# A spectral filter with a gated causal convolution: one convolution block in seven on GpSimd

## The chip, the cores and the metric

The kernel runs on one core of a Trainium2 chip. The metric is the device time of one execution in microseconds; the median of three runs of the kernel before is 308.13 us (307.31 to 309.5). One more execution was recorded by the hardware profiler: it took 308.17 us, and its trace spans 306.3 us from the first to the last instruction.

## What is computed

Eight batches of 3200 x 256 go through a filter in the frequency domain (along the 3200), and then through a gated unit with a causal convolution of five taps, one weight for each tap and channel.

```python
X = np.fft.rfft(x, axis=1)
Y = X * (filt_r + 1j * filt_i)[None, :, :]
y = np.fft.irfft(Y, n=3200, axis=1)
yp = np.concatenate([np.zeros((8, 4, 256)), y], axis=1)
gate_pre = sum(conv_w[k] * yp[:, k:k + 3200, :] for k in range(5))
gate = 1.0 / (1.0 + np.exp(-gate_pre))
out = (gate * (y @ w_val)) @ w_out
```

## The kernel before

The transform of length 3200 is cut into 100 x 32. For each batch the work goes through these stages, named as the tasks in the code are named:

- `lx`: eight loads of x (200 KB each as bf16), issued on GpSimd (line 202), into a pool of ten buffers.
- `s1` / `so`: eight first-stage products on TensorE (line 467), each into a two-bank PSUM area, and their evacuation to the tile `so` by ScalarE or VectorE (lines 458 and 460, the two arms of the helper `copy`).
- `t`: four 32x32 transposes on VectorE (line 486).
- `s2` / `xs` / `z` / `ia` / `ue`: in seven pieces, the second-stage product (line 496), its evacuation `xs`, the multiplication with the filter on VectorE (line 512, `z`, both inputs in SBUF), the first inverse product (line 527) and its evacuation to `u`. The seventh piece is half as wide.
- `wr` / `lv`: from batch 1 on, `u` goes to a scratch in DRAM and comes back in another order as `vt`, with DMAs issued on SyncE (lines 550, 560 and 561). Batch 0 has transposes on VectorE instead (line 568).
- `ib` / `ye`: eight second inverse products (line 578), evacuated by ScalarE to `yt` (line 587), which holds a batch of y, channels on partitions, bf16, with four columns of zeros ahead (`ha`, a memset on GpSimd, line 594).
- Then for each of seven blocks of up to 512 positions (the seventh has 128): `cv`, the convolution as 20 matmuls of 64x64 diagonal weights `dg_t` (line 609); `ga`, its sigmoid on ScalarE from PSUM to `gt` (line 619); `vl`, the value product (line 628); `gv`, gate times value on VectorE (line 643); `op`, the output product (line 651); `oe`, its evacuation to `o`; `st`, the store of 512 KB issued on SyncE (line 666), from a pool of five buffers.

A convolution block needs all eight `ye` of its batch. There are four PSUM areas of two banks for all products. GpSimd cannot hand anything over in PSUM, and in this kernel it only loads, writes constants and makes memsets.

The order on each engine is made when the program is built. `Plan` holds every task with an engine (or two that it may go to), a cost, a rank and what it depends on; `run` goes through an estimated time and gives each free engine the ready task of lowest rank. The rank of a task of batch b is `8 * b + LAG[stage] + STEP[stage] * n`, with `FIRST` added for batch 0; `STAY` and `LEAN` add to the rank where TensorE would change its mode or where VectorE would take a task that ScalarE could take as well. Each engine then runs its list strictly in that order. Instructions on different engines wait for each other through semaphores.

The first 44 us hold the tables that are computed on the chip, the filter's load and batch 0. Batches then overlap: while batch b is convolved, batch b+1 goes through its filter and batch b+2 through its first stage.

Of the kernel before, what the change touches and what calls it, by code (L numbers as in the profile page):

```python
# [20 lines left out]
NV = 4 * NS  # L21
TURN = (0,)

LAG = dict(lx=-36, s1=-112.5, so=-60, t=188, pd=-44.5, s2=33.5, xs=111.5, z=-11, ia=44.5,
           ue=37.5, k=-47, ib=73, ye=38.5, cv=84, ga=-76.5, vl=75, gv=-70.5, op=82, oe=29)
FIRST = dict(lx=-69, s1=32.5, so=44.5, t=56.5, pd=-52, s2=8, xs=4.5, z=-13, ia=-16.5, ue=49.5,
             k=-34, ib=-10.5, ye=10.5, cv=10.5, vl=-27.5, gv=3, op=99.5, oe=-45.5)
CONV = 1.0
STEP = dict(lx=0.25, s1=0.8, so=1.4, t=0.8, s2=1.25, xs=0.4, z=2.35, ue=0.5, k=1.35, ib=0.15,
            ye=1.8, cv=0.1, ga=2.1, vl=0, gv=0.4, op=0.2, oe=0.2)  # L30
STAY, LEAN = 17.5, 12
RC = 4
NCH = R // RC
UCH = [(m, min(2, NM - m)) for m in range(0, NM, 2)]
BLK = 512
NB = 7
MAGIC = 12582912.0
SEM = dict(PE=0.2, ACT=0.13, DVE=0.13, none=0.0)


class Plan:
# [9 lines left out]
    def add(self, name, engines, rank, deps, emit, take=(), give=(), land=0.0, mode=None,  # L51
            ps=0, free=()):
        self.tasks[name] = dict(engines=engines, rank=rank, deps=deps, emit=emit, take=take,
                                give=give, land=land, mode=mode, ps=ps, free=free, slots=[])

    def places(self, n):
        if n == 0:
# [7 lines left out]
    def run(self):  # L65
        left = dict(self.tasks)
        users, need = {}, {}
        for n, t in left.items():
            need[n] = len(t["deps"])
            for d in t["deps"]:  # L70
                users.setdefault(d, []).append(n)
        ready_at = {n: 0.0 for n in left}
        free = {}
        mode = turn = None
        gives = []
        ready = {n for n in left if need[n] == 0}
        order = []
        now = 0.0
        while left:
            gives.sort(key=lambda v: v[0])  # L80
            while gives and gives[0][0] <= now + 1e-9:
                for pool in gives.pop(0)[1]:
                    if isinstance(pool, int):
                        self.slots.append(pool)
                    else:
                        self.room[pool] += 1
            best = None
            for n in ready:
                t = left[n]
                if ready_at[n] > now + 1e-9:  # L90
                    continue
                if self.places(t["ps"]) is None or any(self.room[p] < 1 for p in t["take"]):
                    continue
                for e, cost in t["engines"].items():
                    if free.get(e, 0.0) <= now + 1e-9:
                        away = e == "PE" and t["mode"] != mode
                        other = e == "DVE" and len(t["engines"]) > 1
                        key = (t["rank"] + (self.stay if away else 0.0)
                               + (self.lean if other else 0.0), cost)
                        if e == "DQ":  # L100
                            key = (ready_at[n] + (1e4 if t["mode"] == turn else 0.0), 0.0)
# [36 lines left out]
        return order  # L138
# [3 lines left out]
def kernel(  # L142
# [37 lines left out]
    dg_t = cpool.tile([128, 2, K, 64], BF16, name="dg_t")  # L180
    wv_t = cpool.tile([128, 2, D], BF16, name="wv_t")
    wo_t = cpool.tile([128, 2, D], BF16, name="wo_t")

    dpool = ctx.enter_context(tc.tile_pool(name="scr", bufs=2, space=bass.MemoryType.DRAM))
    pp = ctx.enter_context(tc.tile_pool(name="ps", bufs=1, space=bass.MemoryType.PSUM))
    ps_all = pp.tile([128, 4, 1024], FP32, name="ps")
    NXT = 10
    xpool = ctx.enter_context(tc.tile_pool(name="xin", bufs=NXT))
    sopool = ctx.enter_context(tc.tile_pool(name="s1o", bufs=1))
    tpool = ctx.enter_context(tc.tile_pool(name="s2i", bufs=1))  # L190
# [81 lines left out]
    def load_w():  # L272
        for dh in range(2):
            for r in range(2):
                ch = 128 * dh + 64 * r
                nc.gpsimd.dma_start(
                    out=wv_t[:, dh, :].rearrange("p (r h j) -> p h r j", r=2, h=2)[:, r],
                    in_=moe_w_val[128 * dh:128 * dh + 128, 128 * r:128 * r + 128]
                    .rearrange("p (h j) -> p h j", h=2))
                nc.gpsimd.dma_start(out=wo_t[64 * dh:64 * dh + 64, r, :],  # L280
                                    in_=moe_w_out[ch:ch + 64, :])

    def sp_setup():
        cw = g["cw"] = g1.tile([128, 2, K], FP32, name="cw")
# [9 lines left out]
                                      in_=f_t[p:p + 32, w, :, m0:m1, :])  # L294

    def cf_dve():
        idx = g1.tile([128, 2, 2, 32], FP32, name="idx")
        V.scalar_tensor_tensor(idx[...], g["k1f"][...], g["pcol"][:, 0:1], g["phf"][...],
                               op0=ALU.mult, op1=ALU.add)
        ts(idx[...], idx[...], 0.01, ALU.mult)  # L300
# [301 lines left out]
    def conv(b, c):  # L602
# [9 lines left out]
                                 start=(k == 0), stop=(k == K - 1))  # L612
        st["cv", b, c] = ps

    def gate(b, c):
        ps = st.pop(("cv", b, c))
        g = gpool.tile([128, 2, BLK], BF16, name="gt")
        w = width(c)
        nc.scalar.activation(g[:, :, 0:w], two_banks(ps, w), AF.Sigmoid)  # L619
        st["G", b, c] = g  # L620

    def val(b, c):
# [3 lines left out]
        for eh in range(2):  # L626
            for dh in range(2):
                nc.tensor.matmul(ps[:, 512 * eh:512 * eh + w],  # L628
                                 lhsT=wv_t[:, dh, 128 * eh:128 * eh + 128],
                                 rhs=y[:, dh, H + BLK * c:H + BLK * c + w],  # L630
                                 start=(dh == 0), stop=(dh == 1))
        st["vl", b, c] = ps
# [13 lines left out]
    def outp(b, c):  # L646
        gv_ = st.pop(("GV", b, c))
        ps = psum()
        for a in range(width(c) // 128):
            for eh in range(2):  # L650
                nc.tensor.matmul(ps[:, D * a:D * a + D],  # L651
                                 lhsT=gv_[:, eh, 128 * a:128 * a + 128], rhs=wo_t[:, eh, :],
                                 start=(eh == 0), stop=(eh == 1))
        st["op", b, c] = ps

# [7 lines left out]
    def store(b, c):  # L663
# [4 lines left out]
            in_=o[:, 0:w // 128 * D])  # L668


    plan = Plan(dict(xt=NXT, so=1, t=1, xs=3, z=3, u=1, e=2, v=1, y=2, g=NGB, gv=NGB, o=NOB), 4,
                stay=STAY, lean=LEAN)
    add = plan.add

# [7 lines left out]
    for b in range(B):  # L682
# [65 lines left out]
        add(f"ha{b}", {"POOL": 0.2}, at("ib"), [f"ye{b},0"], lambda e, b=b: halo(b))  # L748
        for c in range(NB):
            f = width(c) / BLK  # L750
            add(f"cv{b},{c}", {"PE": 1.08 * f}, at("cv", c),
                [f"ye{b},{j}" for j in range(NCH)] + [f"ha{b}", "dg0", "dg1"],
                lambda e, b=b, c=c: conv(b, c), ps=1, take=("g",), mode=1)
            add(f"ga{b},{c}", {"ACT": 0.77 * f + 0.16}, at("ga", c), [f"cv{b},{c}"],
                lambda e, b=b, c=c: gate(b, c), free=[f"cv{b},{c}"])
# [14 lines left out]
    add("wts", {"POOL": 5.0}, 8.5, ["hold"], lambda e: load_w())  # L770
# [3 lines left out]
    for n, when in (("fl0", 25.0), ("fl1", 30.0)):  # L774
# [62 lines left out]
```

## Time and profile before

| | |
|---|---|
| median of three runs | 308.13 us |
| the profiled execution | 308.17 us |
| span of its trace | 306.3 us |
| mean granted TensorE clock | 0.975 |
| HBM read, written | 42.08 MB, 38.14 MB |

The groups of instructions that the change touches, or that run beside what it adds (line, engine, operation, out<-in, shape, count; busy us, mean ns of one; idle time before them and what ended it):

```profile
L643 DVE TENSOR_TENSOR gv<-ps,gt 128x1024 bf16<-128x1024 f32 (+1 forms) x56 | 60.7, 1100 | 24.4 <-PE ps L628 17.5
L512 DVE TENSOR_TENSOR z<-xs,f_t 128x2048 bf16<-128x2048 bf16 (+1 forms) x56 | 62.1, 1140 | 1.5 <-DMA f_t<-in_filt_i_dram 0.9
L609 PE MATMUL ps<-yt,dg_t 64*64 64x512 bf16 (+1 forms) x1120 | 60.7, 354 | 0.6 <-ACT yt L587 0.5
...
L619 ACT ACTIVATE gt<-ps 128x1024 bf16<-128x1024 f32 (+1 forms) x56 | 52.0, 944 | 7.7 <-PE ps L609 5.4
...
L202 POOL DMA_DIRECT2D xt<-in_x_dram x64 | 35.4, 557 | 100.5 <-PE ps L467 96.5
```

PE is TensorE's matmuls, PEld its weight loads, DVE is VectorE, ACT ScalarE, POOL GpSimd. A group's mean mixes its full and its short forms. Matmuls are pipelined, so 1120 of 354 ns overlap. An engine's idle time matters only where it is the one that sets the pace.

### The profile page before, as it was taken

What the parts mean: (1) busy time and instruction counts of PE and PEld (TensorE: products, weight loads), DVE (VectorE), ACT (ScalarE), POOL (GpSimd) and SP (SyncE); (2) the same over time, 40 slices, a digit from 0 to 9 for tenths busy, and PEclk for the clock granted to TensorE, in tenths of its full rate; (3) what the DMA queues carried; (4) which work ended last, traced back from release to release, by engine and by line L of the source; (5) the groups of instructions that cost most, each with busy time, mean ns of one, the idle gap of its engine ahead of it and who ended that gap; (6) DMA issues with size and microseconds to landing.
All of it is one profiled execution on the core that took longest, in us unless ns stands there. A gap on an engine that the chain in (4) does not pass through costs nothing.

```text
span 306.3 us, 8876 instructions
## 1 busy us (share of the span) xinstructions
PE 263.4 (86%) x3658; PEld 160.3 (52%) x3684; DVE 255.6 (83%) x284; ACT 254.3 (83%) x301; POOL 58.0 (19%) x120
## 2 busy tenths in 40 slices
PE   2831789889988898999699999998999999999993
PEld 0120526345446446754467447836577676566562
DVE  7688997889999899998399999989999985455442
ACT  3864879999799899997689999999889977786663
POOL 8584467520140050032000210000000000000000
PEclk9999955999999999999999999999999999999998
DMA  6999599998899989999599898858355993947255
GB/s 91 185 161 164 95 183 122 187 189 219 282 218 274 344 161 246 299 268 230 156 286 324 263 218 269 317 204 280 121 190 210 327 333 108 327 162 277 89 208 223
DMA packets 53208, 67.44 MB, mean 220 GB/s; under 512 B 7792, under 2 KB 34032, under 8 KB 53168
## 3 DMA queue, kind: packets, MB, share of 16 engines
q1 hardware_dynamic: 41264, 51.79, 50.4%
q0 software_dynamic: 11904, 15.08, 30.6%
q8 instruction: 29, 0.48, 0.6%
q14 instruction: 11, 0.09, 0.1%
HBM read 42.08 MB, written 38.14 MB: 262 GB/s over the span
## 4 chain that ended last, share of the span: by engine, by line
PE 41%; DVE 20%; DMA 14%; ACT 12%; issue 6%; POOL 4%; SPq 0%; DVEq 0%; ACTq 0%; POOLq 0%
PE ps L609 12%; PE ps L651 10%; PE ps L628 9%; DVE xs L460 6%; DVE z L512 6%; DMA xt<-in_x_dram 5%; PE ps L578 4%; DVE gv L643 4%; DMA escr<-u 4%; ACT yt L587 3%; PE ps L527 3%; ACT so L458 3%; DVE u L460 3%; DMA f_t<-in_filt_r_dram 2%; PE ps L467 2%
## 5 line engine op out<-in xcount | busy, mean ns | idle before, releaser
L643 DVE TENSOR_TENSOR gv<-ps,gt 128x1024 bf16<-128x1024 f32 (+1 forms) x56 | 60.7, 1100 | 24.4 <-PE ps L628 17.5
L512 DVE TENSOR_TENSOR z<-xs,f_t 128x2048 bf16<-128x2048 bf16 (+1 forms) x56 | 62.1, 1140 | 1.5 <-DMA f_t<-in_filt_i_dram 0.9
L609 PE MATMUL ps<-yt,dg_t 64*64 64x512 bf16 (+1 forms) x1120 | 60.7, 354 | 0.6 <-ACT yt L587 0.5
L458 ACT ACTIVATE so<-ps 128x1024 bf16<-128x1024 f32 x55 | 53.7, 1044 | 7.9 <-PE ps L467 5.6
L619 ACT ACTIVATE gt<-ps 128x1024 bf16<-128x1024 f32 (+1 forms) x56 | 52.0, 944 | 7.7 <-PE ps L609 5.4
L587 ACT ACTIVATE yt<-ps 128x800 bf16<-128x800 f32 x64 | 51.4, 852 | 7.0 <-PE ps L578 6.8
L467 PE MATMUL ps<-xt,cf_t 100*128 100x512 bf16 x128 | 45.5, 443 | 11.2 <-DMA xt<-in_x_dram 7.1
L202 POOL DMA_DIRECT2D xt<-in_x_dram x64 | 35.4, 557 | 100.5 <-PE ps L467 96.5
L651 PE MATMUL ps<-wo_t,gv 128*128 128x256 bf16 x400 | 51.8, 272 | 0.6 <-DVE gv L643 0.6
L628 PE MATMUL ps<-yt,wv_t 128*128 128x512 bf16 (+1 forms) x198 | 50.5, 354 | 1.8 <-DVE xs L460 0.3
L458 ACT ACTIVATE o<-ps 128x1024 f32<-128x1024 f32 (+1 forms) x41 | 38.9, 957 | 10.0 <-PE ps L651 9.2
L609 PEld LDWEIGHTS <-dg_t 64*64 64x64 bf16 x1120 | 31.1, 106 | 21.8 <-issue 3.0
L651 PEld LDWEIGHTS <-gv 128*128 128x128 bf16 x400 | 37.0, 97 | 8.7 <-DVE gv L643 1.3
L458 ACT ACTIVATE u<-ps 128x1024 bf16<-128x1024 f32 (+1 forms) x35 | 35.4, 1022 | 7.2 <-PE ps L527 5.4
L486 DVE STREAM_TRANSPOSE tt<-so 128x1024 f32<-128x1024 f32 x32 | 38.4, 1225 | 2.6 <-ACT so L458 2.6
L527 PE MATMUL ps<-z,a_t 64*64 64x256 bf16 x416 | 28.3, 288 | 13.1 <-DVE z L512 9.0
L578 PEld LDWEIGHTS <-vt 104*128 104x128 bf16 (+1 forms) x512 | 30.1, 102 | 9.1 <-issue 2.4
L578 PE MATMUL ps<-ci_t,vt 104*128 104x100 f16 (+1 forms) x512 | 33.9, 214 | 0.7 <-DVE gv L643 0.4
L496 PE MATMUL ps<-tt,w_t 64*64 64x256 bf16 x416 | 23.2, 291 | 9.7 <-DVE tt L486 5.6
L460 DVE CAST xs<-ps 128x1024 bf16<-128x1024 f32 (+1 forms) x27 | 30.7, 1156 | 0.5 <-PE ps L496 0.4
L458 ACT ACTIVATE xs<-ps 128x1024 bf16<-128x1024 f32 (+1 forms) x29 | 27.2, 974 | 4.1 <-PE ps L496 4.1
L628 PEld LDWEIGHTS <-wv_t 128*128 128x128 bf16 x224 | 18.7, 97 | 19.8 <-issue 5.6
(94 smaller groups left out, 192.3 us busy)
## 6 DMA issues: line engine op xcount, KB each, us to landing
out_dram<-o SPq DMA_DIRECT2D x48, 512.0 KB
xt<-in_x_dram POOLq DMA_DIRECT2D x64, 200.0 KB, 7.2
escr<-u SPq DMA_DIRECT2D x42, 256.0 KB
vt<-escr SPq DMA_DIRECT2D x56, 192.0 KB
out_dram<-o SPq DMA_DIRECT2D x8, 128.0 KB
f_t<-f_t SPq DMA_DIRECT2D x4, 224.0 KB
escr<-u SPq DMA_DIRECT2D x7, 128.0 KB
vt<-escr SPq DMA_DIRECT2D x56, 16.0 KB
```

What stands on the lines that cost most here:

```text
L458: nc.scalar.activation(dst, src, AF.Copy, **kw)
L460: nc.vector.tensor_copy(dst, src)
L467: nc.tensor.matmul(ps[:, 512 * h:512 * h + 512], lhsT=cf_t[0:L].rearrange("p h c i -> p (h c i)"), rhs=xv[:, DQ // 2 * h:DQ // 2 * h + DQ ...
L486: nc.vector.transpose(dst, src)
L512: nc.vector.tensor_tensor(z[:, :, :, 0:nm * D], st.pop(("XS", b, u))[:, :, 0:nm * D].unsqueeze(1) .to_broadcast((128, 2, 2, nm * D)), f_t[ ...
L578: nc.tensor.matmul(ps[:, o:o + L], lhsT=v[rows, RC * j + a, 128 * dh:128 * dh + 128], rhs=ci_t[rows, way, :], start=True, stop=True)
L587: nc.scalar.activation(y[:, :, H:H + N].rearrange("p h (a r) -> p h a r", r=R)[:, :, :, RC * j:RC * j + RC], ps[:, :].rearrange("p (h n) - ...
L609: nc.tensor.matmul(ps[64 * dh:64 * dh + 64, 512 * r:512 * r + w], lhsT=dg_t[rows, dh, k, :], rhs=y[rows, dh, BLK * c + k:BLK * c + k + w], ...
L619: nc.scalar.activation(g[:, :, 0:w], two_banks(ps, w), AF.Sigmoid)
L628: nc.tensor.matmul(ps[:, 512 * eh:512 * eh + w], lhsT=wv_t[:, dh, 128 * eh:128 * eh + 128], rhs=y[:, dh, H + BLK * c:H + BLK * c + w], sta ...
L643: nc.vector.tensor_tensor(o, i0, i1, op=ALU.mult)
L651: nc.tensor.matmul(ps[:, D * a:D * a + D], lhsT=gv_[:, eh, 128 * a:128 * a + 128], rhs=wo_t[:, eh, :], start=(eh == 0), stop=(eh == 1))
```

## The change

Block 5 of each batch's seven (positions 2560 to 3071) leaves TensorE. `side` computes it on GpSimd with ten tasks, one for each tap and half of the channels: the first tap of a half multiplies into an fp32 tile `acc` in SBUF, the other four multiply into `tap` and add to `acc`. The gate of that block reads `acc` instead of PSUM. In GpSimd's tile the channels lie in the natural order, not in the order that the diagonal products leave, so the block's value and output products take copies of the two weight matrices in that order (`wvs_t`, `wos_t`), loaded by two more DMAs. There is one `acc`. The pool of output buffers goes from five to four, that of x buffers from ten to nine, and one index tile of the setup is used again instead of a new one. All ranks are other numbers (`LAG`, `FIRST`, `STEP`, `STAY`, `LEAN`), so the order of the tasks changes on every engine; ties are broken by the order in which tasks were added.

```diff
-STAY, LEAN = 17.5, 12
+STAY, LEAN = 21, 102.5
...
+SIDE = [(b, 5) for b in range(8)]
...
-    NXT = 10
+    NXT = 9
...
+        nc.gpsimd.dma_start(out=wvs_t[...], in_=moe_w_val.rearrange("(h p) e -> p h e", h=2))
+        nc.gpsimd.dma_start(out=wos_t[...], in_=moe_w_out.rearrange("(h p) e -> p h e", h=2))
...
-        idx = g1.tile([128, 2, 2, 32], FP32, name="idx")
+        idx = g["phf"]
...
-    NGB, NOB = 3, 5
+    NGB, NOB = 3, 4
...
+    apool = ctx.enter_context(tc.tile_pool(name="acc", bufs=1))
...
+    def side(b, c, n):
+
+        k, dh = n // 2, n % 2
+        if n == 0:
+            st["A", b, c] = apool.tile([128, 2, BLK], FP32, name="acc")
+        w = width(c)
+        acc = st["A", b, c][:, dh, 0:w]
+        src = st["Y", b][:, dh, BLK * c + k:BLK * c + k + w]
+        cw = g["cw"][:, dh, k:k + 1]
+        if k == 0:
+            nc.gpsimd.tensor_scalar(acc, src, cw, None, op0=ALU.mult)
+        else:
+            t = apool.tile([128, BLK], FP32, name="tap")[:, 0:w]
+            nc.gpsimd.tensor_scalar(t, src, cw, None, op0=ALU.mult)
+            nc.gpsimd.tensor_tensor(acc, acc, t, op=ALU.add)
+
     def gate(b, c):
-        ps = st.pop(("cv", b, c))
+        ps = st.pop(("cv", b, c), None)
         g = gpool.tile([128, 2, BLK], BF16, name="gt")
         w = width(c)
-        nc.scalar.activation(g[:, :, 0:w], two_banks(ps, w), AF.Sigmoid)
+        src = st.pop(("A", b, c))[:, :, 0:w] if ps is None else two_banks(ps, w)
+        nc.scalar.activation(g[:, :, 0:w], src, AF.Sigmoid)
         st["G", b, c] = g
...
-                                 lhsT=wv_t[:, dh, 128 * eh:128 * eh + 128],
+                                 lhsT=(wvs_t if (b, c) in SIDE else wv_t)[:, dh, 128 * eh:128 * eh + 128],
...
+            if (b, c) in SIDE:
+                for n in range(2 * K):
+                    add(f"cx{b},{c},{n}", {"POOL": (0.6 if n < 2 else 1.65) * f}, at("cv", c),
+                        [f"cx{b},{c},{n - 1}"] if n else
+                        [f"ye{b},{j}" for j in range(NCH)] + [f"ha{b}"],
+                        lambda e, b=b, c=c, n=n: side(b, c, n), take=() if n else ("g", "acc"))
+                add(f"cv{b},{c}", {"none": 0.0}, 0, [f"cx{b},{c},{2 * K - 1}"], None)
+                add(f"ga{b},{c}", {"ACT": 0.77 * f + 0.16}, at("ga", c), [f"cv{b},{c}"],
+                    lambda e, b=b, c=c: gate(b, c), give=("acc",))
```

In the list of GpSimd's instructions that this gives, the ten tasks of a block stand behind the x loads that were ready earlier, and the next batch's halo memset stands between two of its taps from batch 1 on. On ScalarE the gate of block 5 follows that of block 4 in most batches, and the evacuations of later stages follow it.

More of the change, by code (lines that the diff above doesn't have):

```diff
@@ L22 @@
 TURN = (0,)
[L24 to L27, printed above, removed]
+LAG = dict(lx=-387, s1=-186, so=-13, t=185.5, pd=-128.5, s2=-192, xs=161.5, z=201.5, ia=171.5,
+           ue=106.5, k=-19, ib=223.5, ye=-270, cv=230.5, ga=-154.5, vl=173.5, gv=-296, op=233.5,
+           oe=41)
+FIRST = dict(lx=-45.5, s1=95.5, so=8.5, t=263, pd=36, s2=199.5, xs=-69, z=-136.5, ia=-33,
+             ue=8.5, k=74, ib=186, ye=81, cv=23, ga=-105.5, vl=51, gv=-41, op=187.5, oe=152.5)
 CONV = 1.0
-STEP = dict(lx=0.25, s1=0.8, so=1.4, t=0.8, s2=1.25, xs=0.4, z=2.35, ue=0.5, k=1.35, ib=0.15,
-            ye=1.8, cv=0.1, ga=2.1, vl=0, gv=0.4, op=0.2, oe=0.2)
-STAY, LEAN = 17.5, 12
+STEP = dict(lx=0.4, s1=2.5, so=1.6, t=2.5, pd=1.6, s2=0.6, xs=1.85, z=2.5, ue=1.85, k=0.85,
+            ib=0.9, ye=2.5, cv=0.9, ga=0.25, vl=0.1, gv=0, op=0.75, oe=2.25)
+STAY, LEAN = 21, 102.5
 RC = 4
@@ L53, in add @@
         self.tasks[name] = dict(engines=engines, rank=rank, deps=deps, emit=emit, take=take,
-                                give=give, land=land, mode=mode, ps=ps, free=free, slots=[])
+                                give=give, land=land, mode=mode, ps=ps, free=free, slots=[],
+                                at=len(self.tasks))
     def places(self, n):
@@ L97, in run @@
                         other = e == "DVE" and len(t["engines"]) > 1
-                        key = (t["rank"] + (self.stay if away else 0.0)
-                               + (self.lean if other else 0.0), cost)
+                        key = (round(t["rank"] + (self.stay if away else 0.0)
+                                     + (self.lean if other else 0.0), 6), cost, t["at"])
                         if e == "DQ":
-                            key = (ready_at[n] + (1e4 if t["mode"] == turn else 0.0), 0.0)
+                            key = (round(ready_at[n] + (1e4 if t["mode"] == turn else 0.0), 6), 0.0,
+                                   t["at"])
                         if best is None or key < best[0]:
@@ L182 @@
     wo_t = cpool.tile([128, 2, D], BF16, name="wo_t")
+    wvs_t = cpool.tile([128, 2, D], BF16, name="wvs_t")
+    wos_t = cpool.tile([128, 2, D], BF16, name="wos_t")
     dpool = ctx.enter_context(tc.tile_pool(name="scr", bufs=2, space=bass.MemoryType.DRAM))
@@ L651, in outp @@
                 nc.tensor.matmul(ps[:, D * a:D * a + D],
-                                 lhsT=gv_[:, eh, 128 * a:128 * a + 128], rhs=wo_t[:, eh, :],
+                                 lhsT=gv_[:, eh, 128 * a:128 * a + 128],
+                                 rhs=(wos_t if (b, c) in SIDE else wo_t)[:, eh, :],
                                  start=(eh == 0), stop=(eh == 1))
@@ L668, in store @@
             in_=o[:, 0:w // 128 * D])
-    plan = Plan(dict(xt=NXT, so=1, t=1, xs=3, z=3, u=1, e=2, v=1, y=2, g=NGB, gv=NGB, o=NOB), 4,
+    plan = Plan(dict(xt=NXT, so=1, t=1, xs=3, z=3, u=1, e=2, v=1, y=2, acc=1, g=NGB, gv=NGB, o=NOB), 4,
                 stay=STAY, lean=LEAN)
@@ L750 @@
             f = width(c) / BLK
[L751 to L755, printed above, removed]
+            if (b, c) in SIDE:
[7 more added lines that the diff above has]
+                    lambda e, b=b, c=c: gate(b, c), give=("acc",))
+            else:
+                add(f"cv{b},{c}", {"PE": 1.08 * f}, at("cv", c),
+                    [f"ye{b},{j}" for j in range(NCH)] + [f"ha{b}", "dg0", "dg1"],
+                    lambda e, b=b, c=c: conv(b, c), ps=1, take=("g",), mode=1)
+                add(f"ga{b},{c}", {"ACT": 0.77 * f + 0.16}, at("ga", c), [f"cv{b},{c}"],
+                    lambda e, b=b, c=c: gate(b, c), free=[f"cv{b},{c}"])
             add(f"vl{b},{c}", {"PE": 0.87 * f}, at("vl", c),
@@ L769 @@
     add("pool", {"none": 0.0}, -100, [], None, land=20.0)
-    add("wts", {"POOL": 5.0}, 8.5, ["hold"], lambda e: load_w())
+    add("wts", {"POOL": 6.2}, 8.5, ["hold"], lambda e: load_w())
     for j in range(NCH):
@@ L773 @@
     add("dq", {"DQ": 30.0}, -100, [], None, mode=0)
-    for n, when in (("fl0", 25.0), ("fl1", 30.0)):
+    for n, when in (("fl0", 27.0), ("fl1", 31.0)):
         add(n, {"none": 0.0}, -100, [], None, land=when)
```

## The prediction

> **What bounds the kernel now.** I read the page's slices first, then the busy time by stage, then who waited in each stage, then the ends of the run and the first microseconds in order of time.
>
> ```profile
> PE 263.4 (86%) x3658; PEld 160.3 (52%) x3684; DVE 255.6 (83%) x284; ACT 254.3 (83%) x301; POOL 58.0 (19%) x120
> ...
> PE   2831789889988898999699999998999999999993
> ...
> DVE  7688997889999899998399999989999985455442
> ```
>
> Over the span TensorE, VectorE and ScalarE look alike. By stage they do not (columns: stretch, its length, then busy us of PE, weight loads, DVE, ACT, POOL, clock, DMA share, GB/s):
>
> ```profile
> 44.00:74.00 30.00, 26.53 (x342) 14.36 (x348) 26.30 (x23) 28.69 (x34) 12.61 (x23) 0.86 1.00 179
> 74.00:245.00 171.00, 159.37 (x2378) 100.06 (x2383) 161.60 (x153) 156.10 (x182) 17.23 (x36) 1.00 0.85 248
> 245.00:279.00 34.00, 33.79 (x452) 23.16 (x457) 20.22 (x19) 26.71 (x31) 0.10 (x1) 1.00 0.67 236
> 279.00:306.30 27.30, 21.68 (x269) 13.02 (x264) 10.84 (x12) 14.88 (x16) 0.00 (x0) 0.97 0.48 190
> ```
>
> From 74 to 245 us, where the last z (line 512) ends at 244.8, VectorE is busiest, and all its waits there are three rows, 8.8 us; the rest of its idle time is gaps too short to be a wait:
>
> ```profile
> DVE u L460 <- DMA out_dram<-o: 5.0, 1, 5.0
> DVE gv L643 <- PE ps L628: 2.1, 4, 1.0
> DVE so L460 <- PE ps L467: 1.7, 2, 1.2
> ```
>
> After 245 us VectorE has half its time free and TensorE sets the pace: 99% busy to 279, then the last batch's convolution, value and output products, with short waits between them. So work taken from TensorE is worth something after 245 us and little before.
>
> **What is taken from TensorE.** Eight blocks of 20 matmuls of line 609. The chain of waits shows such a block as 1.08 to 1.21 us, so 8.6 to 9.7 us of TensorE time. In the 171 us stretch this buys only what VectorE waits for TensorE: the rows of 2.1 and 1.7, 3.8 us at most, which I take whole. The blocks also ask eight times less for one of the four PSUM areas; TensorE's waits for an evacuation in that stretch, some 9 us, are idle time of an engine that does not set its pace: nothing.
>
> **What VectorE must do before its last z.** The new ranks reorder everything, so I counted instructions in the built programs. Up to the last z the new order has two more gate products (two at 1.21) and three fewer evacuations (three at 1.22): -1.2; the remaining half-size forms cost 0.6. Net -0.6 us. ScalarE has the same work by then (228 us of row durations in both). Ahead of the last z nothing is shorter by more than this.
>
> **The end.** From the chain and the rows, TensorE needs 0.88 us for an output block (line 651), 0.86 for a value block (628), 1.08 for a convolution block, a quarter of these for the short seventh blocks, and 0.45 for a block of line 578 (0.36 from its start to the next, 0.52 busy). By these, its work after the last but one block of line 527 was 57.3 us, and the run needed 57.5 from the last z to its last evacuation. In the new order 51.0 us stand behind the last block of line 527: fewer convolution blocks, though more of the other three kinds. With 1 us from z to that block and 2 for the last evacuation, 54.0. Gain 3.5 us.
>
> **Small edits.** The two weight copies are two more POOL DMAs in the stretch of 44 to 74, where the DMA share is 1.00. The eight there take 0.72 or 0.52 us and up to 0.57 of waiting each, so the six x loads behind them go 0 to 2.2 us later, and with them the first stage of batch 2, which arrived just in time; I take +1.0. Four output buffers: by the packets in the trace a 512 KB store lands 2.3 to 7.9 us after its issue, and stores four apart were issued at least 7.3 us apart, there with a landing of 3.5. Nothing; a store that landed late would hold ScalarE for the difference. Nine x buffers still hold a batch and one load, issued a batch ahead of use against 7.2 us to landing: nothing; without that cover, up to 7.2 once a batch. The gate reads 128x1024 from SBUF: the nearest row, 1.58 us for 1664 from SBUF, gives 1.0 against 1.04. The reuse of an index tile adds no wait: its one instruction reads that tile and writes it.
>
> **The GpSimd block.** Two multiplies, then eight pairs of multiply and add, 128x512, each waiting for the one before. No such row exists. A multiply: memset of 1536 in 1.40 us is 0.85 ns an element, affine select of 128 in 0.29 gives at most 1.3 beside a fixed 0.13, so 512 take 0.57 to 0.80; I take 0.68. An add with two inputs: not under a multiply (0.57), not over two reads at that pace (1.46); I take the middle, 1.0. With 17 gaps of 0.07 (memset to affine select) a block is 10 x 0.68 + 8 x 1.0 + 1.2 = 16.0 us, ends 11.5 and 20.9. The Trainium skill, "GPSIMD Engine Reference", section "Performance versus the Vector engine", has 4497 ns for an add of 2048 fp32; that is an estimate of 1.12 us here, would make the block 17.0 and, by the price in rival 3, the sum 7 us more.
>
> It must fit between the last yt of its batch and its gate on ScalarE. By the built order ScalarE has 22, 19, 17, 17, 17 and 16 us of work there in batches 0 to 5; in 6 and 7 TensorE has 17.5 and 14.8. Behind the block on GpSimd stand the x loads of a later batch and the next halo memset, both needed a batch later: nothing. Behind the late gate on ScalarE stand so, oe and ye evacuations, for which TensorE waits.
>
> **Shared access with VectorE.** This term decides. In order of time:
>
> ```profile
> 6.51 0.22 POOL L251 MEMSET ident<- 128x128 f32 x1
> ...
> 6.80 0.29 POOL L252 TENSOR_SCALAR_AFFINE_SELECT ident<-ident 128x128 f32<-128x128 f32 x1
> 6.85 1.12 DVE L348 TENSOR_SCALAR vt<-vt 128x1664 f32<-128x1664 f32 x1
> 7.06 1.04 POOL L209 IOTA af<- 128x100 f32 x1
> ...
> 25.71 1.89 DVE L219 TENSOR_SCALAR ix<-ix 128x200 f32<-128x200 f32 x1
> 26.08 1.40 POOL L543 MEMSET u<- 128x1536 bf16 x1
> 27.63 0.26 DVE L223 TENSOR_SCALAR fyx<-ix 128x200 f32<-128x200 f32 x1
> ```
>
> The iota of 100 ends just after line 348 does, though 128 elements took 0.26; line 219 ends just after the memset, though line 223 on the same shape took 0.26. Each engine can hold the other, for 0.8 and 1.6 us. But the memset of 0.22 ran inside a VectorE tensor_tensor (line 345, 4.92 to 6.81), and z, also a tensor_tensor of two SBUF inputs, never took over 1.227 us, although x loads were issued on GpSimd beside some. What was beside them only wrote; a reading GpSimd instruction beside z is not in the trace. So a meeting costs between 0 and a whole GpSimd instruction (1.46). I take that they exclude each other, as in the rows where both engines were seen to stop, at half an instruction on average, weighted by its length: 0.45 us. The Trainium skill, "SBUF — State Buffer", section "Who interferes with whom", says so outright: VectorE with two SBUF inputs and a GpSimd instruction that reads SBUF block each other fully. It speaks against this change, and no run here shows that pair yet; by it the sum below stands, without it the sum is that of rival 1.
>
> How many meet: in the built order 7, 6, 4, 4, 4, 4, 0 and 0 z stand in the windows of batches 0 to 7, 29. GpSimd is busy about 0.8 of a window (16 of some 20), so 29 x 0.8 x 0.45 = 10.4 us, all ahead of the last z on the busiest engine. Each z also holds GpSimd up to 1.22, so a block with four needs 20.9 us; windows of 17 to 19 grow by the 2 us that VectorE loses. Batches 2 to 4 just fit; batch 5 is short by some 3 and batch 7 by 1, half of it hidden: +2.0.
>
> **Sum.** The profiled execution took 308.17 us (span 306.3, 1.9 around it), the median of the runs is 308.13. 308.2 - 3.8 - 0.6 - 3.5 + 1.0 + 10.4 + 2.0 = 313.7.
>
> **Rivals.** (1) No exclusion: z stays at 1.22 beside reading GpSimd work, as beside its memsets and DMA issues. 308.2 - 3.8 - 0.6 - 3.5 + 1.0 = 301.3, or 297.5 to 305 with the bounds of the copies, the pace and the block. For it: 56 undisturbed z; against: the two held rows. The balance tips at 0.3 us a meeting: 301.3 + 23 x 0.3 is the time of before. 0.30. (2) Exclusion, but half as many meetings, because GpSimd is done early or z stands back to back: 301.3 + 5.2 = 306.5. 0.17. (3) The block itself is the bound: every us over 16 makes the gates of seven batches late, since windows are full. At 18, between my value and the upper end: 313.7 + 7 x 2 = 328. For it: the chain of 18 dependent instructions and the windows; against: ScalarE has 14 us of waits between 74 and 245 us in which some of it hides. 0.13. (4) That TensorE does not lose the blocks: its built program has 160 fewer matmuls and 160 fewer weight loads; no chance.
>
> **Numbers.** Forecast 313.7, chance 0.40, its own range 309 to 319. A measurement of this kernel tells about 1%, 3.1 us, from no change: 305.1 to 311.2. Faster: 0.29 of rival 1. Same: rival 2 with 0.14, 0.07 of the forecast, 0.01 of rival 1; 0.22. Slower: the rest, 0.49. The range 300.5 to 322 leaves out most of rival 3 and the lower end of rival 1.
>
> **What would show it.** Mean of z (line 512 before) over 1.4 us with a maximum over 2 where the blocks run shows exclusion; 1.22 throughout shows rival 1. GpSimd's tap pairs at 1.7 us from start to start confirm the block; over 2.2 without z beside them is rival 3, with ScalarE's gate waiting for acc. The last z should end near 252 instead of 244.8, and from there to the last evacuation 54 us. If the last z ends before 245, the forecast is wrong.

## The result and the profile after

The changed kernel takes 410.3 us, the median of four runs (408.12 to 411.53); the kernel before took 308.81 beside it (307.31 to 310.13). The ratio is 1.331, with a 95% interval of 1.3256 to 1.3363. Here and below a ratio leaves out executions in a slower state of the chip, so it need not be the quotient of the medians beside it. The profiled execution took 410.65 us, with a span of 408.6 and a mean granted clock of 0.853.

The page of the changed kernel, busy time first, then the slices that the prediction read:

```profile
PE 272.3 (67%) x3492; PEld 161.4 (40%) x3524; DVE 258.1 (63%) x281; ACT 257.4 (63%) x304; POOL 275.4 (67%) x266
...
PE   3616879827889807996299907995399349908913
...
DVE  8689888936999904998089925995386306403411
...
PEclk9999589977999965999589967999599759967986
```

No engine is much busier than before except GpSimd (58.0 to 275.4 us), and each is now busy for about two thirds of the span. TensorE and VectorE show a hole once a batch, and the clock drops at each hole. TensorE has 166 fewer records of matmuls than before, yet 8.9 us more busy time. By stage (stretch, length, busy us of PE, weight loads, DVE, ACT, POOL, clock, DMA share, GB/s; the last z ends at 311.1):

```profile
74.00:311.00 237.00, 168.10 (x2342) 102.55 (x2367) 168.89 (x155) 160.08 (x186) 152.18 (x125) 0.86 0.65 183
311.00:408.00 97.00, 57.96 (x652) 37.12 (x652) 28.54 (x29) 42.96 (x49) 70.26 (x52) 0.81 0.37 137
```

The stretch in which VectorE set the pace has grown from 171 to 237 us, and in it VectorE is now idle for 68 us. What ended ScalarE's waits (total, times, longest):

```profile
ACT gt L645 <- POOL acc L638: 92.6, 8, 13.9
ACT o L467 <- PE ps L677: 12.6, 14, 3.1
ACT so L467 <- PE ps L476: 11.6, 14, 3.2
```

One row carries nearly all of the loss: eight gates, one a batch, wait 92.6 us for the last add on GpSimd. VectorE's waits are what follows from it: it waits for products and gates behind that gate.

```profile
DVE so L469 <- PE ps L476: 39.9, 7, 11.6
DVE gv L669 <- ACT gt L645: 29.7, 5, 12.8
DVE gv L669 <- PE ps L654: 29.2, 15, 16.1
```

The chain of waits, by engine and by line, and the groups:

```profile
POOL 55%; PE 13%; DMA 9%; issue 8%; ACT 8%; DVE 4%; POOLq 0%; ACTq 0%; SPq 0%; DVEq 0%
...
L637 POOL TENSOR_SCALAR tap<-yt,cw 128x512 f32<-128x512 bf16 x64 | 106.6, 1665 | 5.2
...
L638 POOL TENSOR_TENSOR acc<-acc,tap 128x512 f32<-128x512 f32 x64 | 82.0, 1281 | 5.3
L521 DVE TENSOR_TENSOR z<-xs,f_t 128x2048 bf16<-128x2048 bf16 (+1 forms) x56 | 67.8, 1228 | 12.4 <-ACT xs L467 11.3
L645 ACT ACTIVATE gt<-acc 128x1024 bf16<-128x1024 f32 x8 | 8.4, 1056 | 92.6 <-POOL acc L638 92.6
```

55% of the span is on GpSimd, which had 4%. A multiply takes 1.67 us on average. One block in order of time (start, us), with the gate that waits for it in the next fence:

```profile
172.14 3.11 POOL L634 TENSOR_SCALAR acc<-yt,cw 128x512 f32<-128x512 bf16 x2 [4.92 <-ACT yt L596]
...
185.24 1.56 POOL L637 TENSOR_SCALAR tap<-yt,cw 128x512 f32<-128x512 bf16 x1
186.89 1.28 POOL L638 TENSOR_TENSOR acc<-acc,tap 128x512 f32<-128x512 f32 x1
188.27 1.57 POOL L637 TENSOR_SCALAR tap<-yt,cw 128x512 f32<-128x512 bf16 x1
189.92 1.26 POOL L638 TENSOR_TENSOR acc<-acc,tap 128x512 f32<-128x512 f32 x1
...
198.95 1.26 POOL L638 TENSOR_TENSOR acc<-acc,tap 128x512 f32<-128x512 f32 x1
```

```profile
200.25 1.06 ACT L645 ACTIVATE gt<-acc 128x1024 bf16<-128x1024 f32 x1 [11.59 <-POOL acc L638]
201.21 1.92 ACT L467 ACTIVATE so<-ps 128x1024 bf16<-128x1024 f32 x2
```

The block takes 28.1 us from 172.1 to 200.2, and ScalarE ran out of other work 11.6 us earlier. From tap to tap it is 3.03 us (185.24 to 188.27), and that without a z beside it. Over the eight batches the blocks took 33.3, 31.1, 28.1, 28.1, 28.1, 28.9, 27.1 and 27.1 us, against windows (from the last yt of the batch to the end of ScalarE's earlier work) of 24.3, 17.5, 16.7, 16.7, 16.7, 15.9, 16.5 and 18.6.

### The profile page after: what moved, and what is told of

Its sections match the earlier page's. It is cut to its first block, busy times and chain, and to the rows that moved or that the text cites. A ratio compares the mean times of both kernels' runs of the same rounds, so it can differ in the third digit from the quotient of the medians.

```text
span 408.6 us, 8700 instructions
## 1 busy us (share of the span) xinstructions
PE 272.3 (67%) x3492; PEld 161.4 (40%) x3524; DVE 258.1 (63%) x281; ACT 257.4 (63%) x304; POOL 275.4 (67%) x266
## 4 chain that ended last, share of the span: by engine, by line
POOL 55%; PE 13%; DMA 9%; issue 8%; ACT 8%; DVE 4%; POOLq 0%; ACTq 0%; SPq 0%; DVEq 0%
POOL tap L637 26%; POOL acc L638 20%; DMA xt<-in_x_dram 6%; POOL acc L634 5%; PE ps L677 4%; PE ps L476 4%; POOL xt L208 3%; ACT so L467 2%; ACT yt L596 2%; ACT o L467 2%; PE ps L587 2%; DMA f_t<-in_filt_r_dram 2%; DMA f_t<-in_filt_i_dram 2%; PE ps L505 1%; PE ps L654 1%
## 5 line engine op out<-in xcount | busy, mean ns | idle before, releaser
L637 POOL TENSOR_SCALAR tap<-yt,cw 128x512 f32<-128x512 bf16 x64 | 106.6, 1665 | 5.2
L638 POOL TENSOR_TENSOR acc<-acc,tap 128x512 f32<-128x512 f32 x64 | 82.0, 1281 | 5.3
L645 ACT ACTIVATE gt<-acc 128x1024 bf16<-128x1024 f32 x8 | 8.4, 1056 | 92.6 <-POOL acc L638 92.6
L618 PE MATMUL ps<-yt,dg_t 64*64 64x512 bf16 (+1 forms) x960 | 54.9, 365 | 14.2 <-ACT o L467 13.1
L634 POOL TENSOR_SCALAR acc<-yt,cw 128x512 f32<-128x512 bf16 x16 | 27.6, 1730 | 51.4 <-ACT yt L596 51.2
L467 ACT ACTIVATE so<-ps 128x1024 bf16<-128x1024 f32 x46 | 45.4, 1029 | 11.8 <-PE ps L476 11.6
L467 ACT ACTIVATE o<-ps 128x1024 f32<-128x1024 f32 (+1 forms) x40 | 38.4, 963 | 15.6 <-PE ps L677 12.6
L469 DVE CAST so<-ps 128x1024 bf16<-128x1024 f32 x18 | 21.9, 1220 | 40.2 <-PE ps L476 39.9
L645 ACT ACTIVATE gt<-ps 128x1024 bf16<-128x1024 f32 (+1 forms) x48 | 44.1, 925 | 4.8 <-PE ps L618 3.8
L654 PE MATMUL ps<-yt,wv_t 128*128 128x512 bf16 (+1 forms) x164 | 44.2, 361 | 2.3 <-ACT o L467 0.2
L467 ACT ACTIVATE xs<-ps 128x1024 bf16<-128x1024 f32 (+1 forms) x41 | 38.6, 960 | 5.6 <-PE ps L505 5.4
```

The costliest lines, as they stand in the source:

```text
L467: nc.scalar.activation(dst, src, AF.Copy, **kw)
L618: nc.tensor.matmul(ps[64 * dh:64 * dh + 64, 512 * r:512 * r + w], lhsT=dg_t[rows, dh, k, :], rhs=y[rows, dh, BLK * c + k:BLK * c + k + w], ...
L637: nc.gpsimd.tensor_scalar(t, src, cw, None, op0=ALU.mult)
L638: nc.gpsimd.tensor_tensor(acc, acc, t, op=ALU.add)
L645: nc.scalar.activation(g[:, :, 0:w], src, AF.Sigmoid)
L654: nc.tensor.matmul(ps[:, 512 * eh:512 * eh + w], lhsT=(wvs_t if (b, c) in SIDE else wv_t)[:, dh, 128 * eh:128 * eh + 128], rhs=y[:, dh, H ...
```

## The experiments

All are the changed kernel with the edit shown or named; ratios are to the kernel before on the same chip. The theory was that the block itself is too long and that its late gates make the loss; the rivals were that VectorE and GpSimd hold each other, and that the other edits cost something.

**The first tap alone.** Everything stays but four of the five taps of block 5, which are left out:

```diff
+TAPS = 1
...
-        else:
+        elif k < TAPS:
```

> The changed kernel with only the first tap on GpSimd (two instructions a block instead of 18; the other taps of block 5 are left out of the result), the order on all other engines as in the changed kernel. Late gate (theory): a block of 27 us on GpSimd does not fit between the last yt and the gate, and ScalarE's 92.6 us of waiting for acc are the whole loss; with 3.1 us they are gone and the time is what the rest of the change gives, 300 to 305 us. Rival, the new order and the smaller pools cost something themselves: over 315 us. Rival, exclusion between z and reading GpSimd instructions: also 300 to 305, since only two instructions a batch are left, so this run does not tell it from the theory.

303.24 us (302.1 to 304.77), before 309.89; ratio 0.9841 (0.9759 to 0.9922). Its block takes 3.1 us (5.6 and 4.3 in the first two batches) and no gate waits:

```profile
PE 257.0 (85%) x3492; PEld 155.0 (52%) x3524; DVE 251.7 (84%) x281; ACT 256.1 (85%) x304; POOL 86.9 (29%) x138
```

So the new order, the weight copies, the smaller pools, the index tile and the gate from SBUF together cost less than TensorE's relief brings; without the other four taps the change gains 1.6%, as the prediction's first rival had it. The last z ends at 241.5 and the last evacuation 55.2 us later. The four taps cost 107 us.

**Three taps**, the same edit with `TAPS = 3`; the last two taps are left out:

> Three of the five taps on GpSimd (the other two are left out of the result): 10 instructions, 2 x 1.57 + 4 x (1.57 + 1.28) + gaps = 15.3 us a block, about the 16.0 that the prediction took for the whole block. Late gate alone: windows of 16 to 22 us hold it, no wait over 2 us for acc, 301 to 307 us. With exclusion as the prediction priced it (10.4 us on VectorE, 2.0 of late gates): about 313 us. Gate waits that stay at 5 us or more a batch would mean that the window, not the block, was misjudged.

309.43 us (306.95 to 311.97); ratio 1.0012 (0.9909 to 1.0114). The same kernel again, with more executions, since this interval is wide:

> Three of five taps on GpSimd again (two taps left out of the result), beside the two runs below on the same chip. Late gate: the block of 15 us (up to 20 where z holds it) fits its windows, all waits for acc together about 3 us; 309 us as measured before, so some 6 us over the one-tap kernel that the gate's waits do not explain.

308.23 us (305.3 to 309.87), before 308.29; ratio 0.9986 (0.9956 to 1.0016). A block takes 15.1 us where no z holds it, and its gates wait 3.0 us in all. This block has nearly the length that the prediction gave to the full one (16.0), and the kernel is level with that before: 5 us over the first tap alone. Z reaches 2.31 us beside it in the first profile and 1.78 in the second, and VectorE is busy for 256.9 and 255.9 us against 251.7 with the first tap alone.

**What a tap costs by its form.** Each batch uses another form of the taps after the first; the products are partly other ones (batch 1 uses a constant weight, batch 2 multiplies `acc` instead of y, batches 3 and 5 leave the weight out, batch 4 adds 0.5 to each product, batch 7 computes half a block):

```diff
...
+        if b == 0:
+            G.tensor_scalar(b16, src, cw, None, op0=ALU.mult)
...
+            G.tensor_copy(f32, src)
...
+            G.tensor_scalar(f32, src, cw, 0.5, op0=ALU.mult, op1=ALU.add)
...
+            G.tensor_tensor(f32, src, cw.to_broadcast((128, w)), op=ALU.mult)
```

> Each batch uses another form of GpSimd's tap, to find what makes the multiply 1.57 us (the taps' arithmetic is changed, so the result is not the reference's): batch 0 writes bf16, 1 has a constant instead of a per-partition scalar, 2 reads fp32, 3 is a plain copy to fp32, 4 has two operations, 5 adds yt to acc in one instruction, 6 multiplies with tensor_tensor and a broadcast weight, 7 has half the width. If the per-partition scalar is the cost, the constant of batch 1 falls to about 0.6; if the bf16 input, batch 2 falls; if the software loop per element, batch 7 is about 0.8 and nothing else helps much; if a tensor_tensor is as fast as the add, batch 6 is 1.28.

368.5 us in one run, a mixture of eight forms. GpSimd's groups, each shape by itself (busy us, mean ns of one, then the idle time before them); from the top the multiply with a constant, from fp32, to bf16, as tensor_tensor, at half width, with a second operation, and the copy:

```profile
L643 POOL TENSOR_SCALAR tap<-yt 128x512 f32<-128x512 bf16 x8 | 14.0, 1753 | 0.6
L646 POOL TENSOR_SCALAR tap<-acc,cw 128x512 f32<-128x512 f32 x8 | 13.5, 1682 | 0.6
L640 POOL TENSOR_SCALAR tap<-yt,cw 128x512 bf16<-128x512 bf16 x8 | 12.9, 1608 | 0.6
...
L657 POOL TENSOR_TENSOR tap<-yt,cw 128x512 f32<-128x512 bf16 x8 | 8.3, 1040 | 0.5
L660 POOL TENSOR_SCALAR tap<-yt,cw 128x256 f32<-128x256 bf16 x8 | 7.4, 925 | 0.7
L652 POOL TENSOR_SCALAR tap<-yt,cw 128x512 f32<-128x512 bf16 x8 | 6.6, 829 | 0.6
...
L649 POOL CAST tap<-yt 128x512 f32<-128x512 bf16 x8 | 5.3, 667 | 0.4
```

Means include z that hold them; the medians are 1.50, 1.57, 1.57, 1.04, 0.93, 0.70 and 0.61 us. Neither the type of the input or output nor a constant weight changes the 1.57 us of a multiply with one operation by more than 0.07. The same multiply with a second operation behind it (L652) takes 0.70, and a copy with a cast 0.61. So a pass over 512 elements does run at the pace that the prediction took; the one-operation form does not. Why it is slower than the two-operation form, no row shows.

**The faster form in the whole kernel.** The same result for 0.70 us a multiply, with the order as it was:

```diff
-            nc.gpsimd.tensor_scalar(acc, src, cw, None, op0=ALU.mult)
+            nc.gpsimd.tensor_scalar(acc, src, cw, 0.0, op0=ALU.mult, op1=ALU.add)
...
-            nc.gpsimd.tensor_scalar(t, src, cw, None, op0=ALU.mult)
+            nc.gpsimd.tensor_scalar(t, src, cw, 0.0, op0=ALU.mult, op1=ALU.add)
```

> The full change with one edit: GpSimd's multiply is written as multiply by the weight, then add 0.0, the form that took 0.83 us in place of 1.57 in the run with other forms. The result is that of the changed kernel. Late gate: a block becomes 10 x 0.83 + 8 x 1.28 + 1.5 = 20.0 us, 1.5 to 5 us more where z holds it, against windows of 24, 17.5, 16.7, 16.7, 16.7, 15.9, 16.5 and 18.6: waits of 0, 5, 5, 5, 5, 6, 3.5 and 1.5, about 31 us, on the 303 of one tap and some 6 of exclusion: 330 to 342 us. If the loss were not the block's length but the number of GpSimd instructions or their reads, it would stay near 400.

351.13 us (348.7 to 351.81); ratio 1.1379 (1.1336 to 1.1422). ScalarE's waits and GpSimd's groups:

```profile
ACT gt L645 <- POOL acc L638: 31.1, 8, 6.1
```

```profile
L638 POOL TENSOR_TENSOR acc<-acc,tap 128x512 f32<-128x512 f32 x64 | 86.9, 1358 | 5.3
L637 POOL TENSOR_SCALAR tap<-yt,cw 128x512 f32<-128x512 bf16 x64 | 58.0, 907 | 5.2
```

The block falls from 27.1 to 18.4 us where no z holds it, and 59 us of the loss go with it: 6.8 us for each us of block. The waits came out as expected, the time 9 us above the range expected: 303.2 + 31.1 leaves 16.8. VectorE's busy time is up by 12.6 over the first tap alone, and the mean clock is 0.926; this run does not separate the two.

**GpSimd writes instead of reads.** To separate the length of the block from the shared access, multiplies and adds became memsets of about the same time; the sums are not the reference's. First for all five taps:

```diff
...
+        for i in range(3):
+            nc.gpsimd.memset(t[:, 0:w] if k else acc, 0.25)
+        if k:
+            for i in (w, w, w // 2):
+                nc.gpsimd.memset(acc[:, 0:i], 0.25)
```

> Each multiply is three memsets of 512 fp32, each multiply and add six memsets of about the same time together, so GpSimd is busy about as long and reads nothing from SBUF (the convolution of block 5 is left out of the result). Late gate: the same waits less the 10 us by which z stretched GpSimd's instructions, so at 27 us a block 390 to 403 us, and in proportion if the memsets come out shorter (about 7 us of the time for each us a block). Exclusion as the main cause: z back at 1.22 and under 340 us.

359.59 us in one run. Its time does not answer the question: as nothing read yt, the blocks of batches 2 to 7 started 2 to 16 us before the last yt, and the waits fell to 50.8 us, at least in part for that reason. What it does show is z: 1.225 us at most, all through blocks of 28 to 32 us. In the next the first tap reads yt as before, and only the later ones of three taps are memsets:

> As the three-tap kernel, but the eight instructions of taps 1 and 2 are replaced by memsets of the same total time, which write the same tiles and read nothing (these taps are left out of the result, the first tap stays, so the block still waits for yt). Exclusion theory: the three-tap kernel loses its 6 us because reading GpSimd instructions and z hold each other; without the reads z is back at 1.22 at most beside the memsets and the time at 302 to 305 us. Rival, GpSimd's mere occupation (late x loads and halo memsets behind the block, the window): no change, 308 to 311 us.

Blocks of 14.9 to 16.7 us (21.4 in batch 0), no wait, z at most 1.33 (and that beside the first tap, which reads; beside memsets alone 1.22), VectorE busy 251.7 against 255.9 with real taps. Six runs fell into two groups, 301.5 to 303.3 and 307.5 to 307.9, so its time settles nothing; the 4.2 us of VectorE's time are what the three-tap kernel pays for the shared access. Last, with all five taps:

```diff
+TAPS = 5
...
+        elif k < TAPS:
+            for i in range(3):
+                nc.gpsimd.memset(t[:, 0:w], 0.25)
+            for i in (w, w, w // 4):
+                nc.gpsimd.memset(acc[:, 0:i], 0.25)
```

> What is left to settle is the 14.5 us that the changed kernel takes beyond the kernel with the first tap alone (303.2) and the waits of its eight gates (92.6). Here the first tap of a half is computed as before, the four other multiplies are three memsets of 512 each and the adds memsets of 512, 512 and 128: sums that are not the reference's, in about the same time (2.92 us a pair in the three-tap kernel, so a block of 3.2 + 8 x 2.92 = 26.6 us), starting after the last yt as in the changed kernel, and reading nothing. The gates should wait 26.6 us less the windows of the changed kernel (24.3 and 15.9 to 18.6), 70 us in total, perhaps 80. Theory: 6.4 us of the 14.5 are VectorE held by GpSimd's reads and the rest, about 1 us a wait, is TensorE at half clock after each wait. Then this kernel takes 303 us, its waits, and 6 to 10 us more; z stays under 1.35 us, VectorE is busy 252 us, and the slices after a gate's wait still show a clock of 0.5. Rival: all of the 14.5 is the exclusion. Then the time is 303 us and the waits, within 3 us.

397.54 us (396.94 to 400.15), before 308.86; ratio 1.2922 (1.2808 to 1.3037). The page, z by its shape, and ScalarE's wait:

```profile
PE 273.1 (69%) x3492; PEld 162.4 (41%) x3524; DVE 253.4 (64%) x281; ACT 256.5 (65%) x304; POOL 258.4 (65%) x522
```

```profile
L522 DVE TENSOR_TENSOR z<-xs,f_t 128x2048 bf16<-128x2048 bf16 x48 | 57.8, 1226 | 10.3 <-ACT xs L468 10.2
```

```profile
ACT gt L648 <- POOL acc L641: 82.3, 8, 11.3
```

With z hardly disturbed (1.42 us once beside a first tap, over the 1.35 expected; 1.22 beside memsets alone) the kernel still takes 397.5 us: 303.2, 82.3 of waits, and 12.0 more. The rival, that all of this rest is the exclusion, falls; the rest and the waits are also above the 6 to 10 and the 70 to 80 expected. The slices after a wait show the half clock here too. TensorE is busy 16.1 us longer than with the first tap alone, on the same 3492 records.

**The planner is told.** The faster form, the planner's costs of a tap at 0.95 and 2.45 instead of 0.6 and 1.65, and ranks searched again with these costs:

```diff
-LAG = dict(lx=-387, s1=-186, so=-13, ...
+LAG = dict(lx=-128.8, s1=-324.8, so=-189.0, ...
...
-                    add(f"cx{b},{c},{n}", {"POOL": (0.6 if n < 2 else 1.65) * f}, at("cv", c),
+                    add(f"cx{b},{c},{n}", {"POOL": (0.95 if n < 2 else 2.45) * f}, at("cv", c),
```

> All eight blocks on GpSimd in the faster form (multiply, then add 0.0), and the planner is given what was measured: 0.95 us for a first tap and 2.45 for a later one in place of 0.6 and 1.65, with ranks searched again for these costs, so that the gates of block 5 stand later on ScalarE. Late gate: the 48 us that the faster form still lost came from gates that stood 4 to 6 us too early and what follows from that; without these waits the time is back at 303 to 315 us. If the loss came from GpSimd's work itself (its reads beside z, its occupation), about 330 us or more remain.

317.93 us (317.2 to 321.43), before 306.72; ratio 1.0397 (1.0325 to 1.0469). Windows are now 24 to 33 us and the gates wait 0.7 in all, so the waits are gone; it is still slower than before, and just above the 303 to 315 expected. VectorE's group:

```profile
L517 DVE TENSOR_TENSOR z<-xs,f_t 128x2048 bf16<-128x2048 bf16 x48 | 66.9, 1425 | 0.6 <-ACT xs L463 0.5
```

With the short z the group takes 73.3 us against 62.1 before, 11.2 more on the engine that sets the pace, and the last z ends at 257.6 us, against 244.8 before. The order of the tasks is another one as well, so this run alone does not show that z is the whole of it. The same with a block in every second batch (`SIDE = [(b, 5) for b in (0, 2, 4, 6)]`), ranks searched again:

> The same with only the blocks of batches 0, 2, 4 and 6 on GpSimd, the other four back on TensorE, ranks searched for that. Half of TensorE's relief (4.3 us) and half of the exclusion (2 to 6 us on VectorE): 303 to 312 us, level with the kernel before within 1%.

Two executions took 312.68 and 314.09 us, above the 303 to 312 expected; ratio 1.0211 (1.0156 to 1.0265), z's group 69.3 us. Two more took 317.75 and 858.52 us; what held the last one, nothing on record shows. By the two, half of the blocks cost about half, and neither number of blocks is a gain. Last, the multiply as the change has it, its own ranks, and the planner's costs at 1.66 and 3.05:

> The changed kernel in its own form and with its own ranks, only the planner is given the measured 1.66 and 3.05 us in place of 0.6 and 1.65. Late gate: the gates move back behind other work on ScalarE and most of the 92.6 us of waits goes, but a block of 27 to 33 us and 4.5 us of x loads fill GpSimd for the whole of a batch, whose period was 31 to 34 us in the one-tap kernel; 335 to 365 us, GpSimd the busiest engine in the middle of the run. If wrong costs in the planner were not the link, it stays near 410.

356.47 us (355.28 to 357.65, two runs); ratio 1.1614 (1.1545 to 1.1684). The gates wait 24.3 us, 18.5 of it in the last batch, and VectorE waits 57.6 us for gates. So about half of the loss goes by planning with the true duration; the ranks were not searched again for it, and whether others would do better was not tried. No kernel that computes everything beat the one before.

## Why the prediction was wrong

Forecast 313.7, measured 410.3: slower as it leaned to, but far outside its range.

**The step that failed is the price of a multiply, under "The GpSimd block".** It was put between 0.57 and 0.80 us, at 0.68, from memset and affine select; it takes 1.57. Ten of them make 8.9 us. The add was put at 1.0 and takes 1.27: eight make 2.2. The block is 27.1 us instead of 16.0, beyond the upper end of 20.9. The row that was bent too far is the affine select: it bounds the pace of an element, not every instruction that touches as many. The copy and the two-operation form lie at that pace, and the whole kernel with the latter gets 59 us back. By the page of the Trainium skill that the prediction quoted ("GPSIMD Engine Reference", section "Performance versus the Vector engine"), an add was an estimate of 1.12 us; the trace has 1.27, and the multiply was the larger miss.

**What followed from it was named, as rival 3,** with 0.13 and a price at 18 us only; its sign, pairs of over 2.2 us with no z beside them and a gate that waits for `acc`, is what the trace shows (3.03). Its slope was right: 7 us for each us of block, measured 6.8 from 18.4 to 27.1. Its formula at 27.1 gives 391.4, and at 18.4 it gives 330.5 where 351 was measured, so it starts some 20 us too low at both. At 18.4 some 12 of these are waits: 31.1, where the formula has 2.0 + 7 x 2.4 = 18.8, since the blocks with four z took 21.4 in windows of 17. Of the other 8, 1.9 are the kernel with the first tap alone against rival 1's sum (303.2 against 301.3); the rest lies between what VectorE lost and a cost that no step had, that of a wait beyond itself (next paragraph), and that run does not separate them.

**The sum** is 303.2 (first tap alone) + 92.6 (gates) + 14.5. With writes in place of the reads the 14.5 is 12.0, so what waits of this length cost beyond themselves is about 1.5 us each. Of the 10.3 us by which the waits differ (92.6 against 82.3), some 4 are the memsets' shorter blocks (26.65 us against 27.11 where no z is beside them, eight of them); the other 6, and the 2.5 left of the 14.5, are put down to the reads, as a remainder and not as a measurement.

**Point by point.** With the first tap alone, what VectorE and the end gain (-3.8, -0.6, -3.5, +1.0) came out as a sum: rival 1's 301.3 against 303.2; the last z would end at 244.8 - 3.4 = 241.4 and ended at 241.5; the end took 55.2 against 54.0. The -3.8 was luck: from 74 us to the last z VectorE still waits 4.7 us for TensorE (3.8 before), and what went is the wait of 5.0 us for a store, which the prediction had left standing. No cost of the small edits put at nothing shows, and the gate at 1.0 (1.06) was right; the +1.0 for the copies can't be told apart in that. The windows, 22, 19, 17, 17, 17, 16, 17.5 and 14.8 by the built order, were right within 2.3 but for the last (18.6). With late gates the end took 91.9 us instead of 54, and the last z ended at 311.1 instead of 252.

**The exclusion was right in kind, and its size depends on the form of the multiply.** Z goes up to 2.3 us beside adds, and beside memsets alone it stays at 1.22, as the section of the Trainium skill that the prediction quoted ("SBUF — State Buffer", "Who interferes with whom") has it for instructions that read. The 10.4 us are close to what the form nearest to the forecast costs: with multiplies of 0.70 us, VectorE is busy for 12.6 us longer than with the first tap alone, and 11.4 of these are z (the faster form, then the first tap alone):

```profile
L521 DVE TENSOR_TENSOR z<-xs,f_t 128x2048 bf16<-128x2048 bf16 (+1 forms) x56 | 74.6, 1350 | 3.9 <-ACT xs L467 3.6
...
L522 DVE TENSOR_TENSOR z<-xs,f_t 128x2048 bf16<-128x2048 bf16 (+1 forms) x56 | 63.2, 1147 | 0.3 <-ACT xs L468 0.2
```

With the slow multiply it is less: 6.4 us of VectorE's time in the changed kernel, and 4.2 with three taps. Two places of the changed kernel, in order of time, suggest why:

```profile
60.73 2.35 DVE L521 TENSOR_TENSOR z<-xs,f_t 128x2048 bf16<-128x2048 bf16 x2
60.88 3.54 POOL L634 TENSOR_SCALAR acc<-yt,cw 128x512 f32<-128x512 bf16 x1
...
65.55 1.57 POOL L637 TENSOR_SCALAR tap<-yt,cw 128x512 f32<-128x512 bf16 x1
65.95 1.37 DVE L521 TENSOR_TENSOR z<-xs,f_t 128x2048 bf16<-128x2048 bf16 x1
```

The first multiply started behind a z and had to let two of them pass: 3.54 = 1.57 + 1.97. The second had begun 0.40 us ahead of a z and held it for only 0.15. I had charged half of the instruction; a multiply of this form seems to hold z for its first 0.55 us (an estimate: 0.40 + 0.15), and the rest of its 1.57 us goes on beside it. An add holds z nearly to its end: the z of 2.30 us began 0.04 us behind an add of 1.27. So here the two did not block each other for the whole of every instruction.

## What to carry to other kernels

Before work is moved to an engine that has not done it in the trace, measure that one instruction in its exact form, since two forms of the same product differed here by 1.57 against 0.70 us, and a bound from a neighbouring instruction held for one of them only. A helper engine's chain of dependent steps is compared with the window between its last input and its first reader: below it the chain is free but for shared access, above it every us is paid once a batch, and the planner must know the true duration. Even with the waits planned away, taking eight blocks of 1.1 us from TensorE went with 11 us more on VectorE, so price the move on the engine that sets the pace.

## What the runs showed of the hardware

- On GpSimd, 128x512 bf16 to fp32, undisturbed: multiply with one operation 1.57 us, with a second operation 0.70, copy with cast 0.61, multiply by a broadcast tile as tensor_tensor 1.04; an add of two fp32 tiles 1.27. Half the width of the first takes 0.93, so it is some 0.28 us and 2.5 ns an element.
- After each wait TensorE runs at half clock for a while. The changed kernel and two of its waits, which end at 200.2 and 245.3 (columns as above; the clock stands before the last two):

```profile
188.00:200.20 12.20, 2.41 (x23) 0.87 (x22) 4.05 (x4) 0.66 (x1) 11.51 (x11) 0.70 0.09 28
200.20:204.00 3.80, 1.74 (x12) 0.73 (x12) 0.09 (x1) 3.75 (x4) 1.12 (x3) 0.50 0.62 96
204.00:208.00 4.00, 4.00 (x19) 2.12 (x18) 2.67 (x3) 1.14 (x3) 1.10 (x2) 0.67 0.57 111
208.00:212.00 4.00, 3.63 (x28) 2.14 (x27) 4.00 (x4) 4.00 (x5) 1.66 (x3) 1.00 1.04 185
...
245.30:249.00 3.70, 1.60 (x11) 0.62 (x11) 0.00 (x0) 3.62 (x4) 0.04 (x1) 0.50 0.00 0
249.00:253.00 4.00, 4.00 (x22) 2.37 (x20) 2.84 (x3) 1.50 (x3) 0.00 (x0) 0.75 0.10 39
253.00:257.00 4.00, 3.63 (x27) 2.13 (x27) 4.00 (x4) 4.00 (x5) 0.00 (x0) 1.00 0.56 223
```

  Two shorter stretches, just before the clock falls for the first of these waits and just before it rises again:

```profile
189.56:192.97 3.41, 0.90 (x10) 0.32 (x9) 2.75 (x3) 0.00 (x0) 3.19 (x5) 1.00 0.12 35
...
203.21:206.62 3.41, 3.41 (x13) 1.81 (x12) 1.38 (x2) 1.84 (x2) 0.55 (x1) 0.50 0.62 93
```

  A clock of 0.67 or 0.75 over the second stretch is 0.5 for its first 2 to 2.7 us, so half clock lasts some 6 us after a wait, though TensorE is busy throughout that stretch; and the same 3492 records take 272.3 us instead of 257.0. The Trainium skill, "TensorE: Matmul & The Clock Gate", Part 1, states half rate after an idle window of about 3.4 us and full rate after about 3.4 us of sustained work. The trace agrees on the way up (full clock from 206.62, behind 3.41 us of work throughout); on the way down, half clock set in behind a stretch that was not wholly idle (0.90 us busy of 3.41). A wait of about 10 us cost some 1.5 us beyond itself in the run with memsets. The 3.41 us of work at half clock can account for that (some 1.7 us lost, an estimate), but no run keeps the clock up, so that the clock is the reason is argued and not shown.
